# A chunked recurrence with a feed-forward block behind it: another order of operations, a spread by 128-row products, whole-half stores and an early flag

## The chip, the cores and the metric

One core of one Trainium2 chip runs the whole kernel. The metric is device time in microseconds (us) of that core, as the median of several runs. The engines are TensorE (PE, products; its weight loads are listed as PEld), VectorE (DVE), ScalarE (ACT), GpSimd (POOL) and SyncE (SP, which here issues nearly all transfers). Everything is float32.

## What is computed

```python
# r, k, v, w, a, b: (batch 4, heads 8, 768 tokens, 40)
state = zeros((B, H, D, D))
for t in range(S):
    y[:, :, t] = einsum('bhd,bhde->bhe', r_t, state)
    Sa = einsum('bhde,bhe->bhd', state, a_t)
    state = state * w_t[:, :, None, :] - einsum('bhd,bhe->bhde', Sa, b_t)
    state = state + einsum('bhd,bhe->bhde', v_t, k_t)
x = y as (B*S = 3072 tokens, H*D = 320)
h = x @ w_in                  # 320 -> 2048
out = (h * sigmoid(h)) @ w_out    # 2048 -> 320
```

## The kernel before

The 768 tokens are cut into 12 chunks of 64. Within a chunk the recurrence is turned into products and the inverse of a triangular matrix for each of the 32 pairs of batch and head, so that the state moves on once for each chunk. The feed-forward block of a chunk (256 tokens over the four batches) then follows.

The work is a list of some 1400 operations, each of one engine. They are written down by steps: `prepare(n)` (DVE scans L476 and L494 for the decays, scaling L503, the second operand L507, products L526, their mask L591, turning by L631, products L606), `special(n)` for the first two chunks (the triangular inverse on DVE and PE: dots L657 and L658, the spread L734, gather L785, both L842, turn L855, products L887 and DVE sums L902, three rounds of them), `chain(n)` (L1041, L1051, solve L1066, L1096, L1126, L1153, L1169), `read(n)` (look L1199 with its mask L1211, L1238, L1253, scaling L1264), `bring(n)` (the transfer of the scaled result through `xh` to `xt`, L1283, L1344 and L1346), and `moe(n)` (L1356 and L1369 make 2048 features from 320, L1379 is the silu on ACT, L1396 is the second product in two output halves of four parts each, L1408 copies a half out of PSUM, L1411 stores it). `inverse(k)` and `merge(k)` (L968, L994) serve two later chunks together: its dots on DVE, transfers md to mi and zd to ZQ through DRAM, and then products with ZQ. `weights(u)` for u = 0 to 9 turns the 64-bit weights into float32 on DVE and ACT (L339 to L357), with products by L363 for the first three.

No scheduler sorts these steps when the program is built. The table `ORDER` lists all operations in one fixed sequence, and each engine gets its own in that sequence. The table `SLOTS` gives to each stretch of PSUM use one of four `pair` tiles or one of two `lam` tiles. An operation waits for the data that it reads and for the users of the tile that it overwrites. SP issues transfers in its own order as well, and where one waits, those behind it on SP wait too.

L734, the spread, takes the inverse's parts to another layout: for each of 16 positions, two products of 64 rows, with `fold` as the right operand, a view into the output buffer `ot`. ACT then copies the result to `xs` in one instruction.

There is a fallback: `guard()` counts on DVE how many entries of a check are in range, adds them over the partitions by one product (L1435), and writes a flag `bad` (L1438). All engines load the flag (L1488) and branch (L1489) around a slow general version. The guard is the last thing on the list, so DVE writes the flag behind the last copy.

Of the kernel before, what the change touches and what calls it, by code (L numbers as in the profile page):

```python
# [129 lines left out]
01001320111001013332100203211223101103303113201032131321222203130311323300300330021021001012012012122003033032  # L130
02110122311301200033321330210003311032122012123032031001303022012221221111213030021331311012031301020012032100
3301311002232331201021233230133211001311001001320012311102301202201130032012312121031300312032
# [4 lines left out]
def kernel(  # L137
# [69 lines left out]
    wc = ring("wc", 3, Q)  # L207
    ot = ring("ot", 1, DM)
    pairs = [ps.tile([128, 2, 512], F32, name=f"pair{i}") for i in range(4)]
    lams = ring("lam", 2, Q * C)  # L210
    ms, zs = (dr.tile([128, 16, 16], F32, name=x) for x in ("ms", "zs"))
    few = ZQ.rearrange("p q t -> p (q t)")
    fold, own, mine = ot[0][:, 288:304], ot[0][:, 304:308], ot[0][:, 308:312]
    xh = [dr.tile([DM, T], F32, name=f"xh{i}") for i in range(NN)]
    md = [dr.tile([128, 32, 32], F32, name=f"md{i}") for i in range(2)]
    xd = [dr.tile([128, 32, 32], F32, name=f"xd{i}") for i in range(2)]
    zd = [dr.tile([2, 32, 32, 32], F32, name=f"zd{i}") for i in range(2)]

    plan = Plan({"pair": pairs, "lam": lams})
# [1401 lines left out]
```

## Time and profile before

| what | us |
|---|---|
| three runs | 693.54, 689.51, 689.6 |
| median | 689.6 |
| profiled execution, whole | 695.31 |
| its span, first to last instruction | 693.3 |
| PE busy in it | 651.6 |
| DVE, ACT, POOL busy | 386.5, 209.4, 6.5 |
| largest groups on PE: L1396, L1356, L1369 | 220.7, 174.0, 47.3 |
| first product starts | 13.98 |
| last product of the kernel ends | 684.77 |

The profiled execution is 5.7 us above the median of the runs; its span leaves 2.0 us of its time outside. The parts of a profile used here are the page (busy shares, 40 slices of the span, the chain of work that ended last), a table of stages, the timeline of one engine, and groups of instructions by line. In a timeline row stand start, duration, engine, line, operation, destination and source, and in brackets the idle time before it with what ended it. A float32 product shows as two records, so "x8" of L1396 is four products. "issue" is time in which an engine waited for nothing that the profile shows.

### The profile page before, as it was taken

How to read it: one execution, taken by the hardware profiler on the slowest of the kernel's cores; microseconds unless marked ns; L12 is line 12 of the kernel's file. 1: busy time of each engine (PE TensorE's matmuls, PEld its weight loads, DVE VectorE, ACT ScalarE, POOL GpSimd, SP SyncE). 2: the span in 40 equal slices, each digit the busy share in tenths (PEclk: the TensorE clock that was granted, in tenths of full speed). 3: DMA queues.
4: the chain of work that ended last, by engine and by line, in shares of the span. 5: the costliest groups of instructions: out<-in, count | busy, mean ns of one | idle time of the engine just before them, and what ended most of it. 6: DMA issues, size and time to landing. Idle time of an engine off the chain costs nothing.

```text
span 693.3 us, 26090 instructions
## 1 busy us (share of the span) xinstructions
PE 651.6 (94%) x12150; PEld 521.7 (75%) x12150; DVE 386.5 (56%) x558; ACT 209.4 (30%) x285; POOL 6.5 (1%) x21
## 2 busy tenths in 40 slices
PE   1799997999999999999999999999989999999995
PEld 1576785787788787888688788788778787787773
DVE  7899988798353952665934727961628611202000
ACT  4455535034324033323034224044113033131020
POOL 2000000100000000000000000000000000000000
PEclk9999999999999999999999999999999999999998
DMA  9934756426453254542734651453350431301001
GB/s 323 276 82 128 195 156 191 127 77 139 119 131 95 61 152 97 150 105 64 160 94 105 178 119 57 124 135 81 90 117 24 121 93 31 92 13 50 16 8 23
DMA packets 113711, 76.27 MB, mean 110 GB/s; under 512 B 61884, under 2 KB 109820, under 8 KB 112956
## 3 DMA queue, kind: packets, MB, share of 16 engines
q1 hardware_dynamic: 113596, 74.54, 41.1%
q8 instruction: 96, 1.57, 1.0%
q14 instruction: 19, 0.16, 0.1%
HBM read 60.16 MB, written 14.35 MB: 107 GB/s over the span
## 4 chain that ended last, share of the span: by engine, by line
PE 83%; DMA 7%; SPq 4%; DVE 2%; issue 2%; ACT 1%; DVEq 0%
PE pair L1396 28%; PE pair L1356 22%; PE pair L1369 6%; PE pair L1199 4%; PE pair L1253 3%; PE pair L526 3%; PE pair L363 2%; PE pair L1153 2%; DMA vu<-in_v 2%; PE pair L606 2%; PE pair L631 2%; PE pair L1238 2%; PE pair L1041 2%; PE pair L1066 1%; DMA kbv<-in_bT 1%
## 5 line engine op out<-in xcount | busy, mean ns | idle before, releaser
L1396 PE MATMUL pair<-wo,gts 128*128 128x320 f32 x768 | 220.7, 441 | 2.1 <-issue 2.1
L1396 PEld LDWEIGHTS pair<-wo,gts 128*128 128x128 f32 x768 | 143.6, 191 | 59.8 <-issue 4.0
L1356 PE MATMUL pair<-xt,wi 128*128 128x256 f32 x768 | 174.0, 383 | 1.6 <-DMA xt<-xh 1.6
L1356 PEld LDWEIGHTS pair<-xt,wi 128*128 128x128 f32 x768 | 144.5, 191 | 23.4 <-DVE XI L657 2.0
L1379 ACT ACTIVATE gts<-pair 128x1024 f32<-128x1024 f32 x48 | 47.3, 1020 | 60.7 <-PE pair L1369 59.8
L1211 DVE TENSOR_TENSOR lam<-pair,ml 128x1024 f32<-128x1024 f32 x22 | 26.2, 1220 | 69.7 <-PE pair L1199 69.7
L658 DVE TENSOR_REDUCE XI<-XI 128x64 f32<-128x512 f32 (+9 forms) x85 | 58.7, 690 | 2.9
L657 DVE TENSOR_TENSOR XI<-XI,mi 128x1024 f32<-128x1024 f32 (+8 forms) x60 | 33.6, 560 | 41.7 <-DMA mi<-md 40.5
L1408 DVE COPY ot<-pair 128x320 f32<-128x320 f32 x24 | 11.7, 486 | 74.1 <-PE pair L1396 65.0
L1369 PE MATMUL pair<-xt,wi 64*128 64x256 f32 x384 | 47.3, 387 | 0.0
L526 PE MATMUL pair<-a,kb 40*64 40x64 f32 x1536 | 28.8, 228 | 15.7 <-DVE a L503 14.0
L526 PEld LDWEIGHTS pair<-a,kb 40*64 40x64 f32 x1536 | 26.1, 142 | 19.5 <-issue 16.5
L1369 PEld LDWEIGHTS pair<-xt,wi 64*128 64x128 f32 x384 | 35.3, 189 | 4.9 <-issue 1.0
L507 DVE TENSOR_TENSOR kb<-kbv 128x1024 f32<-128x1024 f32 x24 | 29.1, 1216 | 10.8 <-DMA kbv<-in_kT 5.3
L1199 PEld LDWEIGHTS pair<-r,vut 40*64 40x64 f32 x1536 | 24.9, 136 | 10.0 <-issue 7.4
L1199 PE MATMUL pair<-r,vut 40*64 40x64 f32 x1536 | 27.2, 222 | 5.1 <-issue 2.8
L253 ACT COPY vu<-pair 64x640 f32<-64x640 f32 x22 | 15.1, 687 | 55.0 <-PE pair L1096 54.7
L930 ACT COPY mi<-XI 128x1024 f32<-128x1024 f32 x5 | 10.0, 1992 | 62.6 <-DVE XI L658 59.8
L476 DVE TENSOR_TENSOR_SCAN kbv<-wz,zt 128x1024 f32<-128x1024 f32 x12 | 27.5, 2292 | 1.0
L494 DVE TENSOR_TENSOR_SCAN wz<-wz,zt 128x1024 f32<-128x1024 f32 x12 | 27.4, 2285 | 0.1
L644 ACT COPY kt<-pair 128x640 f32<-128x640 f32 x24 | 16.3, 693 | 31.0 <-PE pair L631 30.9
L657 DVE TENSOR_TENSOR XI<-XI,xs 128x1024 f32<-128x1024 f32 (+1 forms) x25 | 25.2, 1008 | 0.6
(154 smaller groups left out, 637.3 us busy)
## 6 DMA issues: line engine op xcount, KB each, us to landing
wz<-in_wT SPq DMA_DIRECT2D x12, 512.0 KB
a<-in_aT SPq DMA_DIRECT2D x12, 512.0 KB
kbv<-in_bT SPq DMA_DIRECT2D x12, 512.0 KB
kbv<-in_kT SPq DMA_DIRECT2D x12, 512.0 KB
vut<-in_vT SPq DMA_DIRECT2D x48, 96.0 KB
r<-in_rT SPq DMA_DIRECT2D x48, 96.0 KB
vu<-in_v SPq DMA_DIRECT2D x24, 160.0 KB
out<-ot SPq DMA_DIRECT2D x48, 80.0 KB
```

The lines of the kernel that those rows point to most:

```text
L476: nc.vector.tensor_tensor_scan(back(V), back(W[:, 2 : 2 + Q * C]), zt, 1.0, ALU.mult, ALU.add)
L494: nc.vector.tensor_tensor_scan(Z, Z, zt, 0.0, ALU.mult, ALU.add)
L507: TTn[engine].tensor_tensor(out=at_(kb, m0, (m1 - m0, 2), (2 * C, 8), (1, C)), in0=at_((kf, bf)[is_b], 0, (8 * C, 2), (C, 8), (1, C)), in1 ...
L526: nc.tensor.matmul(room.tile[half(h), j, g * C : g * C + C], lhsT=kb[rows(j), place(is_b, q) : place(is_b, q) + C], rhs=A[rows(j), q * C : ...
L657: nc.vector.tensor_tensor(out=at_(tmp, 0, *dims), in0=x, in1=y, op=ALU.mult)
L658: nc.vector.tensor_reduce(out=out_, in_=at_(tmp, 0, *dims), axis=AX.X, op=ALU.add)
L1199: nc.tensor.matmul(pl.tile[half(1 - m if role else m), b, c * C : c * C + C], lhsT=vut[rows(b), role, hu, :], rhs=rs[rows(b), hh, :], star ...
L1211: lambda pl=pl, la=la: nc.vector.tensor_tensor(out=la.tile.rearrange("p (q t) -> p q t", q=Q), in0=pl.tile.rearrange("p a b -> p (a b)").r ...
L1356: nc.tensor.matmul(rooms[g].tile[:, f // 2, (f % 2) * T : (f % 2) * T + T], lhsT=wi[:, k, (4 * g + f) * 128 : (4 * g + f) * 128 + 128], rh ...
L1369: nc.tensor.matmul(rooms[g].tile[:, h, (f % 2) * T : (f % 2) * T + T], lhsT=wi3[half(h), g * 256 + (f % 2) * 128 : g * 256 + (f % 2) * 128 ...
L1379: nc.scalar.activation(out=gts[:, 4 * g * T : 4 * g * T + 4 * T], in_=rooms[g].tile.rearrange("p a b -> p (a b)"), func=AF.Silu)
L1396: nc.tensor.matmul(po[b].tile[:, 0, 0:DM], lhsT=g4[:, f, 128 * b : 128 * b + 128], rhs=wo[:, f, :], start=f == 0, stop=f == NF - 1,)
```

## The change

`ORDER` and `SLOTS` are new, the result of another search (1418 operations before, 1395 now). Five edits come with them.

1. The spread does 16 products over all 128 rows in place of 32 products over 64. `fold` gets a tile of its own of 128 x 2 x 16, zero outside two blocks (one more memset on POOL, two sums over 64 partitions on DVE for one over 128). The result stands in the lower 64 partitions, and two ACT copies of 64 x 256 bring it to `xs`.
2. `own` and `mine`, two other small operands, move within `ot`.
3. Each output half goes out in one transfer of 160 KB in place of two of 80 KB, so 24 stores for 48.
4. The guard is listed ahead of the third part of the last output half, and that part is made to depend on the flag.
5. The last output half is copied by ACT and its store is issued by ACT.

Lines of the kernel after are 4 to 10 higher than before for the same operation.

```diff
 ORDER = """
-0 6 2 1 102 127 7 9 8 10 14 103 128 3 11 17 15 25 129 104 16 26 130 18 105 41 106 27 139 71 67 114 4 115 65 5 63 131
+0 6 128 1 3 2 7 129 8 9 10 130 14 11 131 12 13 15 23 25 71 103 284 4 104 132 77 133 105 106 27 26 24 134 17 115 116
...
-    fold, own, mine = ot[0][:, 288:304], ot[0][:, 304:308], ot[0][:, 308:312]
+    own, mine = ot[0][:, 288:292], ot[0][:, 292:296]
+    fold = sb.tile([128, 2, 16], F32, name="fold")
...
+        nc.gpsimd.memset(fold, 0.0)
+        for b in range(2):
+            x = ident[half(b)].rearrange("p (g s) -> p s g", s=16)
+            nc.vector.tensor_reduce(out=fold[half(b), b], in_=x, axis=AX.X, op=ALU.add)
...
                 for t in range(16):
-                    for b in range(2):
-                        nc.tensor.matmul(
-                            pr.tile[half(b), 0, 16 * t : 16 * t + 16],
-                            lhsT=at_(XI[half(b)], 64 * t, (1, 64)),
-                            rhs=fold[half(b)],
+                    nc.tensor.matmul(
+                        pr.tile[half(0), 0, 32 * t : 32 * t + 32],
+                        lhsT=at_(XI, 64 * t, (1, 64)),
+                        rhs=fold.rearrange("p b s -> p (b s)"),
...
-                lambda: nc.scalar.copy(
-                    out=xs.rearrange("p (s t) -> p s t", s=16), in_=pr.tile[:, 0, 0:256].rearrange("p (t s) -> p s t", t=16)
-                ),
+            for b in range(2):
...
+                    lambda b=b: nc.scalar.copy(
+                        out=xs[half(b)].rearrange("p (s t) -> p s t", s=16),
+                        in_=pr.tile[half(0), 0].rearrange("p (t b s) -> p b s t", t=16, b=2)[:, b],
+                    ),
...
-            add("DVE", vec(320), lambda b=b: nc.vector.tensor_copy(out=ot[0], in_=po[b].tile[:, 0, 0:DM]), [po[b]], ["ot"], 10 * n, [po[b]])
-            for m in range(2):
-                r0 = (2 * m + b) * S + C * n
-                dma(lambda m=m, r0=r0: nc.sync.dma_start(out[r0 : r0 + C, :], ot[0][half(m)]), 80, ["ot"], [("out", n, b, m)], 10 * n + 9)
+                if n == NN - 1 and b == 1 and part == 2:
+                    guard()
+                last_ = ["bad"] if n == NN - 1 and b == 1 and part == 2 else []
...
+            e = "ACT" if n == NN - 1 and b else "DVE"
+            add(e, vec(320), lambda b=b, e=e: copy(e, ot[0], po[b].tile[:, 0, 0:DM]), [po[b]], ["ot"], 10 * n, [po[b]])
+            dst = out.rearrange("(m b s) c -> b m s c", m=2, b=2)[b, :, C * n : C * n + C]
+            q = nc.scalar if e == "ACT" else nc.sync
+            dma(lambda q=q, dst=dst: q.dma_start(dst, ot[0]), 160, ["ot"], [("out", n, b)], 10 * n + 9, "ACT" if e == "ACT" else "SP")
...
-    guard()
```

What the new order does is seen at three places. In the rows, a number behind a tile's name is its buffer (`a_82` belongs to chunk 3 here, `a_84` to chunk 2), and "x16" counts instructions.

The first is DVE between the second and the third sum of `special(1)`, L902 before (L908 after), where `prepare(3)` is also under way. Before:

```order
L902 TENSOR_TENSOR XI<-pair_113,X_94 128x1024
L494 SCALAR_TENSOR_TENSOR wz_73<-wz_73,zt 128x1024
L495 MEMSET zt 128x16
L339 TENSOR_SCALAR wo<-wo 128x1024
L503 TENSOR_TENSOR a_82<-a_82,wz_73 128x1024
L342 TENSOR_SCALAR raw_136<-raw_136 128x1024
L507 TENSOR_TENSOR kb<-kbv 128x2x8x64
L902 TENSOR_TENSOR X_94<-pair_111,X_94 128x1024
```

And after:

```order
L908 TENSOR_TENSOR XI<-pair_111,X_94 128x1024
L346 TENSOR_SCALAR raw_137<-raw_137 128x1024
L343 TENSOR_SCALAR wo<-wo 128x1024
L478 TENSOR_SCALAR w_77<-wz_73,pad 128x16
L479 MEMSET wz_73 128x16
L480 SCALAR_TENSOR_TENSOR kbv<-wz_73,zt 128x1024
L908 TENSOR_TENSOR X_94<-pair_113,X_94 128x1024
L345 SCALAR_TENSOR_TENSOR wo<-raw_137,wo 128x1024
```

The second scan of `prepare(3)` (L494), its scaling (L503) and one of its L507 stood ahead of the third sum; only the first scan (L480, which was L476) stands there now, and the rest of that step comes later.

The second is PE in the same stretch, from the third round of `special(1)` to the first L1396 (L1402 after) of the first feed-forward block. Before:

```order
L1356 MATMUL pair_110<-xt,wi 128x256 x8
L887 MATMUL pair_111<-XI 64x64 x32
L631 MATMUL pair_113<-ident,kb 128x40 x16
L1369 MATMUL pair_112<-xt,wi_67 128x256 x4
L1369 MATMUL pair_110<-xt,wi_67 128x256 x4
L526 MATMUL pair_113<-a_82,kb 64x64 x32
L1066 MATMUL pair_111<-X_94,R_91 40x64 x32
L1199 MATMUL pair_112<-r,vut 64x64 x32
L1199 MATMUL pair_113<-r,vut 64x64 x32
L1396 MATMUL pair_111<-wo,gts 128x320 x4
```

And after:

```order
L893 MATMUL pair_113<-XI 64x64 x32
L1362 MATMUL pair_111<-xt,wi 128x256 x8
L1072 MATMUL pair_112<-X_94,R_91 40x64 x32
L635 MATMUL pair_113<-ident,kb 128x40 x16
L1375 MATMUL pair_110<-xt,wi_67 128x256 x4
L1375 MATMUL pair_111<-xt,wi_67 128x256 x4
L1205 MATMUL pair_112<-r,vut 64x64 x32
L1205 MATMUL pair_113<-r,vut 64x64 x32
L1402 MATMUL pair_111<-wo,gts 128x320 x8
```

The block of L1356 moved from ahead of the third L887 to behind it, the turn (L631) and the remainder of the features (L1369) moved from ahead of the solve (L1066) to between it and the look (L1199), and the L526 of chunk 3 is now behind the first L1396.

The third is the end of SP's list. Before:

```order
L1344 DMA xt<-xh_129 128x2x256
L1411 DMA out<-ot_109 64x320
L1346 DMA xt<-xh_129 64x256
L1411 DMA out<-ot_109 64x320 x2
L1346 DMA xt<-xh_129 64x256
L1411 DMA out<-ot_109 64x320 x6
L1488 TENSOR_LOAD bad
L1488 ISA x2
L1489 COMPARE_AND_BRANCH
```

And after:

```order
L1289 DMA xh_130<-lam_114 40x4x256 x2
L1497 TENSOR_LOAD bad
L1497 ISA x2
L1350 DMA xt<-xh_130 128x2x256
L1352 DMA xt<-xh_130 64x256
L1421 DMA out<-ot_109 2x64x320
L1352 DMA xt<-xh_130 64x256
L1421 DMA out<-ot_109 2x64x320 x2
L1498 COMPARE_AND_BRANCH
```

The load of the flag moved from behind all stores to ahead of the last loads of `xt` and the last three stores that SP issues; the last store of all is no longer SP's.

More of the change, by code (lines that the diff above doesn't have):

```diff
@@ L74 @@
 ORDER = """
[52 rows of a table removed]
[51 rows of a table added]
 """
 SLOTS = """
-01001320111001013332100203211223101103303113201032131321222203130311323300300330021021001012012012122003033032
-02110122311301200033321330210003311032122012123032031001303022012221221111213030021331311012031301020012032100
-3301311002232331201021233230133211001311001001320012311102301202201130032012312121031300312032
+03032120310310103031113322130113030313031321012120133302233203100302120300030113122221301002313031103311122222
+00100132320321013011100300311032300031101031201111110203120312213322011300113010023031121123130320221101023303
+2001230013120210211030030211133011012222110103012320100322011112102101010220331321031101320133
 """
@@ L286, in once @@
             nc.gpsimd.tensor_copy(out=ot[0][rows(j), 112 + D * j : 112 + D * j + D], in_=ident[rows(j), rows(j)])
-        for x, axes in ((fold, "p (g s) -> p s g"), (own, "p (b c s) -> p c b s"), (mine, "p (g c) -> p c g")):
-            sizes = dict(s=16) if x is fold else dict(b=2, c=4) if x is own else dict(c=4)
+        nc.gpsimd.memset(fold, 0.0)
+        for b in range(2):
+            x = ident[half(b)].rearrange("p (g s) -> p s g", s=16)
+            nc.vector.tensor_reduce(out=fold[half(b), b], in_=x, axis=AX.X, op=ALU.add)
+        for x, axes in ((own, "p (b c s) -> p c b s"), (mine, "p (g c) -> p c g")):
+            sizes = dict(b=2, c=4) if x is own else dict(c=4)
             nc.vector.tensor_reduce(out=x, in_=ident.rearrange(axes, **sizes), axis=AX.XY if x is own else AX.X, op=ALU.add)
@@ L725, in special @@
         turned = few[:, 256:512]
-        xsk = ["xs"]
+        xsk = [("xs", 0), ("xs", 1)]
         if n in RELAY:
@@ L732, in spread @@
                 for t in range(16):
-                    for b in range(2):
-                        nc.tensor.matmul(
-                            pr.tile[half(b), 0, 16 * t : 16 * t + 16],
-                            lhsT=at_(XI[half(b)], 64 * t, (1, 64)),
-                            rhs=fold[half(b)],
-                            start=True,
-                            stop=True,
-                        )
-            add("PE", 1.9, spread, XIk, [pr], pri, [pr], 64)
-            add(
-                "ACT",
-                act(256),
-                lambda: nc.scalar.copy(
-                    out=xs.rearrange("p (s t) -> p s t", s=16), in_=pr.tile[:, 0, 0:256].rearrange("p (t s) -> p s t", t=16)
-                ),
-                [pr],
-                ["xs"],
-                pri,
-                [pr],
-            )
+                    nc.tensor.matmul(
+                        pr.tile[half(0), 0, 32 * t : 32 * t + 32],
+                        lhsT=at_(XI, 64 * t, (1, 64)),
+                        rhs=fold.rearrange("p b s -> p (b s)"),
+                        start=True,
+                        stop=True,
+                    )
+            pr.left = 3
+            add("PE", 1.9, spread, XIk, [pr], pri, [pr], 64)
+            for b in range(2):
+                add(
+                    "ACT",
+                    act(256),
+                    lambda b=b: nc.scalar.copy(
+                        out=xs[half(b)].rearrange("p (s t) -> p s t", s=16),
+                        in_=pr.tile[half(0), 0].rearrange("p (t b s) -> p b s t", t=16, b=2)[:, b],
+                    ),
+                    [pr],
+                    [("xs", b)],
+                    pri,
+                    [pr],
+                )
         else:
@@ L758, in special @@
                 [("ms", b, c) for b in range(2) for c in range(4)],
-                ["xs", ("in", "S", n)],
+                [*xsk, ("in", "S", n)],
                 pri,
@@ L1406, in moe @@
                 need = sorted({("wo", c) for c in range(4 * part * DM // WS, ((4 * part + 4) * DM - 1) // WS + 1)})
-                add("PE", 2.14, partial(second, b, part), [("gts", part), ("ff", n), *need], [po[b]], pri + 4 + b + part * 0.1, [po[b]], 16, shape="F")
-            add("DVE", vec(320), lambda b=b: nc.vector.tensor_copy(out=ot[0], in_=po[b].tile[:, 0, 0:DM]), [po[b]], ["ot"], 10 * n, [po[b]])
-            for m in range(2):
-                r0 = (2 * m + b) * S + C * n
-                dma(lambda m=m, r0=r0: nc.sync.dma_start(out[r0 : r0 + C, :], ot[0][half(m)]), 80, ["ot"], [("out", n, b, m)], 10 * n + 9)
+                if n == NN - 1 and b == 1 and part == 2:
+                    guard()
+                last_ = ["bad"] if n == NN - 1 and b == 1 and part == 2 else []
+                add("PE", 2.14, partial(second, b, part), [("gts", part), ("ff", n), *need, *last_], [po[b]], pri + 4 + b + part * 0.1, [po[b]], 16, shape="F")
+            e = "ACT" if n == NN - 1 and b else "DVE"
[3 more added lines that the diff above has]
+            dma(lambda q=q, dst=dst: q.dma_start(dst, ot[0]), 160, ["ot"], [("out", n, b)], 10 * n + 9, "ACT" if e == "ACT" else "SP")
     def ahead(step, n):
```

101 rows, old and new, of the table ORDER are left out of this document.

## The prediction

> **What bounds the kernel now.** I read the page first: the busy shares, the tenths and the chain that ended last.
>
> ```profile
> PE 651.6 (94%) x12150; PEld 521.7 (75%) x12150; DVE 386.5 (56%) x558; ACT 209.4 (30%) x285; POOL 6.5 (1%) x21
> PE   1799997999999999999999999999989999999995
> DVE  7899988798353952665934727961628611202000
> PE 83%; DMA 7%; SPq 4%; DVE 2%; issue 2%; ACT 1%; DVEq 0%
> ```
>
> TensorE (PE) is busy 94% of the span. Only PE work taken away, or idle PE time closed, can shorten this kernel. The 1 in PE's first slice, the 7 in its second and seventh and the 5 in its last show where idle time lies. Beside the first and the seventh, VectorE (DVE) shows 7 to 9: DVE sets the pace there. So I cut the span into stages (busy time of PE, PEld, DVE, ACT, POOL, then granted clock, DMA share, GB/s).
>
> ```profile
> 0.00:14.00 14.00, 0.02 (x3) 0.05 (x3) 10.15 (x29) 5.14 (x5) 4.05 (x17) 1.00 0.90 308
> 14.00:52.00 38.00, 31.69 (x764) 25.01 (x768) 33.87 (x56) 19.93 (x26) 0.00 (x0) 1.00 0.74 197
> 52.00:83.00 31.00, 30.93 (x618) 23.03 (x612) 30.16 (x51) 16.88 (x23) 0.52 (x1) 1.00 0.59 159
> 83.00:119.00 36.00, 28.66 (x680) 24.82 (x681) 30.38 (x36) 16.12 (x19) 0.00 (x0) 0.91 0.60 178
> 340.00:510.00 170.00, 164.61 (x3274) 132.05 (x3273) 92.47 (x124) 51.23 (x75) 0.00 (x0) 0.99 0.46 115
> 684.70:693.30 8.60, 0.09 (x2) 0.00 (x0) 0.54 (x2) 0.00 (x0) 0.00 (x0) 0.69 0.13 28
> ```
>
> PE's idle time is 14.0 us before the first product, 6.3 up to 52, 7.3 between 83 and 119, 5.4 between 340 and 510, and 8.5 behind the last product: 41.5 of the 41.7 us that PE is not busy (693.3 - 651.6). Any gain has to come out of these five places or out of PE's own work.
>
> **The change, part by part.** *Tile-shape changes.* Four products of L1396 between blocks of their own shape, and between others, in the chain:
>
> ```profile
> 245.68 2.15 PE pair L1396 x8
> 161.64 2.35 PE pair L1396 x8
> ```
>
> A change of shape at both ends costs 0.20 us. I counted the places in PE's row of work where the tile's shape changes: 211 before, 211 after. The new order only shifts them among shapes, with changes into 128x128 falling from 73 to 62 and into 64x128 rising from 40 to 47. I take 0; the bounds are plus or minus 1 us (ten changes at 0.10).
>
> *The spread.* Thirty-two products of 64 rows (64 records) against sixteen of 128 rows; for the new ones the nearest row is L1253, which also has 128 rows and 64 records:
>
> ```profile
> 18.10 3.59 PE L734 MATMUL pair<-ot,XI 64*64 64x16 f32 x64
> 227.32 1.79 PE pair L1253 x64
> ```
>
> By L1253, sixteen products take half of 1.79, or 0.9; by L734's own pace they would take 1.8. I take 0.9, 2.7 less than now. It lies at 18 us, where DVE paces the work (33.9 of 38 us busy), so on the end it gives 0, at most 2.7. In place of one copy ACT does two, and DVE does two half-height sums for one; what they add at 18 us (under 1 us) lies in the same place, and I net it with the spread's gain.
>
> *The order between 83 and 119 us.* This is where most of it must come from. PE, then DVE:
>
> ```profile
> 83.40 0.69 PE L855 MATMUL pair<-ident,mi 64*128 64x64 f32 x16
> 85.20 1.16 PE L842 MATMUL pair<-mi,sb 64*64 64x64 f32 x64 [1.11 <-ACT X L253]
> 87.49 3.43 PE L887 MATMUL pair<-X,XI 64*64 64x64 f32 x62 [1.13 <-ACT XI L253]
> 97.51 3.72 PE L1356 MATMUL pair<-xt,wi 128*128 128x256 f32 x16
> 101.16 2.08 PE L887 MATMUL pair<-XI 64*64 64x64 f32 x64
> 103.69 1.97 PE L1369 MATMUL pair<-xt,wi 64*128 64x256 f32 x16
> 106.88 1.16 PE L526 MATMUL pair<-a,kb 40*64 40x64 f32 x64 [1.22 <-DVE kb L507]
> 107.93 1.10 PE L1066 MATMUL pair<-X,R 64*40 64x64 f32 x64
> 110.18 1.61 PE L1199 MATMUL pair<-r,vut 40*64 40x64 f32 x91 [1.04 <-ACT vut L255]
> 114.63 1.14 PE L1199 MATMUL pair<-r,vut 40*64 40x64 f32 x33 [2.84 <-issue]
> 115.70 4.59 PE L1396 MATMUL pair<-wo,gts 128*128 128x320 f32 x12
> ```
>
> ```profile
> 91.03 1.23 DVE L902 TENSOR_TENSOR XI<-pair,X 128x1024 f32<-128x1024 f32 x1 [1.56 <-PE pair L887]
> 97.63 1.23 DVE L902 TENSOR_TENSOR XI<-pair,X 128x1024 f32<-128x1024 f32 x1 [0.85 <-PE pair L887]
> 98.77 2.28 DVE L494 TENSOR_TENSOR_SCAN wz<-wz,zt 128x1024 f32<-128x1024 f32 x1
> ...
> 105.51 1.22 DVE L507 TENSOR_TENSOR kb<-kbv 128x1024 f32<-128x1024 f32 x1 [1.99 <-DMA kbv<-in_bT]
> 106.66 1.22 DVE L902 TENSOR_TENSOR X<-pair,X 128x1024 f32<-128x1024 f32 x1
> ```
>
> The third L902 could have run at 103.2, when the third L887 ended; it ran at 106.7, because the scan of L494, the L503 after it and an L507 that waits 1.99 us for a load stand ahead of it on DVE. Now they stand behind it. I follow the new order on PE. Ahead of L855 a block of L1369 (2.0) and one of L631 (0.5) are gone, and the block before may start up to 2.0 earlier, so L855 runs at 78.9 to 80.9. From there to the first L902 it is 7.6 as before, and 0.9 more because a block of L1369 now stands in the wait of 1.13: 87.4 to 89.4, and I take 88.4. Then L1356 (3.7) and L887 (2.1): second L902 at 94.2. L631 and L526 (1.6) cover it, then L887: product ready at 97.9. DVE, with a scan still ahead, gets to the third L902 at 99.3. PE does an L1356 meanwhile and reaches L1066 at 101.6, with no wait. L631, L1369 (0.5 and 2.0) now stand between L1066 and L1199, and cover the wait of 1.04. L1396 then starts at 101.6 + 1.1 + 2.5 + 2.0 = 107.2, against 115.70. One L526 block (1.07) that was ahead comes later: the lead is 8.5 - 1.1 = 7.4, and 7 as I take it. If the 2.84 us stop, for which the trace shows no releaser ("issue"), comes back, it is 4.6; if L855 is at its early end and L1396 runs at its usual pace (12 records 3.5 instead of 4.59), 9.5. Bounds 4.6 to 9.5.
>
> The clock in this stage was 0.91, and the L1396 behind the 2.84 us stop is 1.1 us slow. The Trainium skill, "TensorE: Matmul & The Clock Gate", Part 1, has the clock fall to half after an idle window of about 3.4 us. Here a stop of 2.84 us, with 1.04 some 1.6 us before it, was enough. By the page's rule stops under 3.4 us would leave the clock whole, and the sum would be 1.1 us lower; the trace does not bear that out.
>
> *The later order.* Idle time between 340 and 510 is a load and one more such stop:
>
> ```profile
> 337.41 8.17 DMA xt<-xh
> 504.00 2.15 issue
> ```
>
> I find as much PE work between L1253 and the next L1356 after the change as before, or more, so I leave these 5.4 us as they are: plus or minus 4.
>
> *Stores.* Half as many issues on SP; SP is not on the path outside the last stage, so 0.
>
> *The end.* Copy, the two stores' issue, flag load, SP's wait for its own branch, and the DMA share in the second after:
>
> ```profile
> 684.77 0.49 DVE L1408 COPY ot<-pair 128x320 f32<-128x320 f32 x1 [5.97 <-PE pair L1396]
> 685.29 1.11 SPq L1411 DMA_DIRECT2D out<-ot  x2
> L1488 SPq TENSOR_LOAD <-bad x1: 737/737/737, 686.5 to 686.5; - x1
> SPq L1489 <- SPq L1489: 2.5, 1, 2.5
> 686.50:687.50 1.00, 0.00 (x0) 0.00 (x0) 0.00 (x0) 0.00 (x0) 0.00 (x0) 1.00 0.78 172
> ```
>
> The chain is copy, issues 1.11, flag load 0.74 behind them, branch 2.5, and then 3.2 us of closing waits. Now SP loads the flag long before the end and has no last store to issue, so its branch can be done early. ACT copies (no row of ACT for this size; I take DVE's 0.5, at most 0.7) and issues (half of 1.11): 1.2 us after PE's end. The data move mostly up to 687.5, which is 2.2 us after the first issue and 1.7 after the second's start; I take 2.5. With the 3.2 of closing waits that makes 6.9 instead of 8.6. I take a gain of 2; the bounds are 0.5 (ACT pays the branch of 2.5 too, behind its flag load) and 3.5 (part of the closing waits overlaps).
>
> Two waits are added there. SP's load of the flag stands ahead of the last loads of xt and of three stores. The flag follows one tiny DVE operation behind the last L1264, which the transfers to xh ahead of it on SP wait for anyway, so 0. PE's third part of the last output half now waits for the flag as well, with more than 30 us of L1356, L1369 and L1396 between the flag's product and it, so 0. There is one buffer ot: ACT's copy has to wait until the store of the other half has read it, and only 4.5 us of L1396 (eight products, 16 records) lie between the two copies at the least. Against copy, issue and 2.2 us for the data (3.3) that holds with about 1 us to spare; should it not, some tenths of the gain go.
>
> The Trainium skill, "DMA: Bandwidth & Descriptors", "Issuing engines are not separate DMA queues", says that issuing from another engine only saves the sequencer's issue time. By that alone the sum's last term would be 0.6. In the rows above the flag load of 0.74 and the branch of 2.5 stood behind the issue on SP too, which is why I take more.
>
> **Sum.** -7 (start) + 0 (shapes) + 0 (spread) + 0 (later) - 2 (end) = -9. The profiled execution took 695.3 us (span 693.3 and 2.0 outside), which is 5.7 above the median of 689.6; I apply the difference to the median: 680.6.
>
> **Rivals.**
> *The lead is eaten by a new wait.* The next thing late would be the merge of the inverse:
>
> ```profile
> 129.81 0.16 DVE L657 TENSOR_TENSOR XI<-XI,mi 128x4 f32<-128x4 f32 x1
> 168.81 0.75 PE L968 MATMUL pair<-ZQ,sb 32*32 32x32 f32 x64
> ...
> L968 PE MATMUL pair<-ZQ,sb 32*32 32x32 f32 x640 | 7.5, 194 | 0.5 <-DMA ZQ<-zd 0.5
> ```
>
> That chain takes up to 39.0 us from its first dot to L968. After the change PE gets to L968 at 107.2 + 53.1 (as from 115.7 to 168.8) = 160.3. PE ends the block that L1264 waits for some 8 us after L1396's start (4.5 of L1396 and about 3.4 of three small blocks), and eight other DVE operations of about 1 us each follow L1264 before the dots, which so start near 124.5. With two weight steps fewer among the dots (2.3 us) the chain ends near 161. It is level, so a small slip in the load of mi or of the weights makes PE wait. If that or the stop of 2.84 takes 4 to 5 of the 7 us, the time is 685 (683 to 688), within 1%. Chance 0.25.
>
> *The change doesn't do what it says.* It counts shape changes, and they are as many as before; if DVE's order matters less than I read, only the end gains: 687.6. Chance 0.08.
>
> *Slower.* The five merges all come late. Summing the durations of PE's blocks between them, the distance from an inverse's last L526 to its merge falls from 56 to 46 us for the first and from 62 to 52 for the second. If each of five merges waits over 1.8 us, the gain of 9 is gone; at 4 us each it is 20 - 9 = 11 slower, 700. Against it: before, L968 waited 0.5 us in all. Chance 0.08.
>
> **How the numbers follow.** My forecast, 680.6, has 0.59, its own range is 676 to 684. The range of 8 in 10 is 674 (lead 9.5, end 3.5, later idle 3 less) to 689.5, which takes in the first two rivals. One per cent, 6.9 us, is about what a measurement of this kernel can tell from no change: under 682.7 is faster. From my forecast nearly all (0.56) and a little of the first rival (0.04) lie there: 0.60; slower 0.08; the rest 0.32.
>
> **What would show it.** Right: the first L1396 starts near 107 (105 to 111); the third L902 ends before PE's L1356 does; PE's idle time between 83 and 119 falls from 7.3 to under 3; 510 on stays solid; behind the last product 6 to 7 us. Wrong: a PE wait on ZQ at the first L968, a long "issue" ahead of L1396, or L855 waiting for mi. A PE busy time that fell by more than 3 us would show that shape changes did matter.

## The result, and the profile after

The kernel after takes 715.98 us (median; 715.12 to 721.07) against 689.63 us before: a ratio of 1.038, with a 95% interval of 1.033 to 1.043. It is slower by 3.8%. A ratio here is an estimate over the fast runs of both kernels, and need not be the quotient of two medians. The profiled execution took 715.12 us, with a span of 713.4.

The busy shares and the slices of the page of the kernel after:

```profile
PE 658.7 (92%) x12118; PEld 529.4 (74%) x12118; DVE 384.5 (54%) x558; ACT 210.0 (29%) x287; POOL 6.3 (1%) x22
PE   1979999999998999989999899988999999999993
PEclk9999999999999999989999899998999999999998
```

PE is busy for 7.1 us more (658.7 against 651.6) and idle for 54.7 us (713.4 - 658.7) instead of 41.7. Between its first and last slice the kernel before had three slices under 9, two of them near the start (the 2nd and the 7th). Now five slices with an 8 are scattered from the 13th to the 28th. Two stages of the kernel before that are needed beside those shown above, and then the stages of the kernel after:

```profile
170.00:340.00 170.00, 169.85 (x3546) 136.98 (x3545) 96.38 (x140) 50.59 (x76) 0.00 (x0) 1.00 0.45 109
510.00:684.70 174.70, 174.70 (x2482) 139.44 (x2480) 46.84 (x64) 33.77 (x45) 0.00 (x0) 1.00 0.20 52
```

```profile
83.00:119.00 36.00, 34.45 (x771) 28.52 (x768) 34.31 (x40) 20.92 (x24) 0.00 (x0) 1.00 0.62 184
170.00:340.00 170.00, 161.28 (x3357) 132.20 (x3358) 94.52 (x136) 47.51 (x71) 0.00 (x0) 0.96 0.42 109
340.00:510.00 170.00, 162.40 (x3121) 131.18 (x3122) 85.33 (x113) 47.21 (x68) 0.00 (x0) 0.96 0.42 107
510.00:705.00 195.00, 188.28 (x2683) 149.38 (x2674) 53.11 (x77) 37.12 (x51) 0.00 (x0) 1.00 0.20 52
705.00:713.40 8.40, 0.00 (x0) 0.00 (x0) 0.00 (x0) 0.00 (x0) 0.00 (x0) 0.59 0.07 20
```

Between 83 and 119 us PE's idle time fell from 7.3 to 1.6 us and the clock rose to 1.00: the start got better. From 170 us on PE loses 8.7, 7.6 and 6.7 us in stages that had lost 0.2, 5.4 and 0 before (of the 6.7, 2.5 lie behind its last product, which ends at 702.5). In the first two of them the granted clock is 0.96, where it had been 1.00 and 0.99. The timeline of PE after, at the place that carried the sum:

```profile
99.23 1.10 PE L1072 MATMUL pair<-X,R 64*40 64x64 f32 x64
104.95 1.20 PE L1205 MATMUL pair<-r,vut 40*64 40x64 f32 x66 [1.10 <-issue]
106.08 4.57 PE L1402 MATMUL pair<-wo,gts 128*128 128x320 f32 x16
```

The first L1402 starts at 106.1, where L1396 started at 115.7. So the lead was won, and lost later. The waits of DVE name where. In the table of waits stand engine, line and releaser, total, number and the longest one; before, then after:

```profile
DVE ot L1408 <- DMA out<-ot: 8.9, 2, 5.5
```

```profile
DVE ot L257 <- DMA out<-ot: 47.0, 8, 10.0
```

L257 is now the line of the copy into `ot`. It waits for the store of the half before it, 47.0 us in all. DVE's waits as such cost nothing where PE has work. But PE now waits for that very copy four times, 4.6 us in all, which the table of the kernel before does not have:

```profile
PE pair L974 <- DVE ot L257: 1.7, 1, 1.7
PE pair L1362 <- DVE ot L257: 1.4, 1, 1.4
...
PE pair L1205 <- DVE ot L257: 1.1, 1, 1.1
...
PE pair L635 <- DVE ot L257: 0.4, 1, 0.4
```

The timelines of DVE and SP after show one such store from end to end, in a quiet place:

```profile
670.78 0.49 DVE L257 COPY ot<-pair 128x320 f32<-128x320 f32 x1 [21.07 <-issue]
677.13 0.49 DVE L257 COPY ot<-pair 128x320 f32<-128x320 f32 x1 [5.86 <-DMA out<-ot]
```

```profile
671.30 0.58 SPq L1421 DMA_DIRECT2D out<-ot  x1
```

From the issue at 671.30 to the release of `ot` at 677.13 pass 5.8 us. The view of the DMA engines from 671 to 678 us, in 40 slices of 0.175 us (tenths of the 16 engines busy), tells how:

```profile
DMA  0000000011012571111110111111111110000000
```

Apart from a short burst, the load of `xt`, one tenth of the sixteen engines is busy for four microseconds: about two engines pass the 128 rows of 1280 bytes one after another.

The trace also keeps the time of each update of the semaphores by which transfers report that they have landed. They bear out the two engines for this store, and show what it does to a transfer behind it. A transfer of 64 rows (in the kernel with two stores, below) makes 16 updates. This one makes three: one at 672.26, ahead of the first slice in which an engine is busy, and two at 677.00 and 677.01. The load of `xt` that SP issued right behind it, at 671.97, makes 14 of its 16 updates between 673.83 and 675.04 and the last two at 677.30 and 677.32, just behind the store's two. In the kernel with two stores the same load was issued at 650.44 and had all 16 by 652.67. So two parts of a load that has nothing to do with the store stand behind it: the load lands after 5.3 us in place of 2.2.

### The profile page after: what moved, and what is told of

It is laid out like the page before. It is cut to its first block, busy times and chain, and to the rows that moved or that the text cites. A ratio compares the mean times of both kernels' runs of the same rounds, so it can differ in the third digit from the quotient of the medians.

```text
span 713.4 us, 26003 instructions
## 1 busy us (share of the span) xinstructions
PE 658.7 (92%) x12118; PEld 529.4 (74%) x12118; DVE 384.5 (54%) x558; ACT 210.0 (29%) x287; POOL 6.3 (1%) x22
## 5 line engine op out<-in xcount | busy, mean ns | idle before, releaser
L1402 PE MATMUL pair<-wo,gts 128*128 128x320 f32 x768 | 219.6, 441 | 0.1
L1402 PEld LDWEIGHTS pair<-wo,gts 128*128 128x128 f32 x768 | 144.5, 192 | 58.8 <-issue 2.9
L1362 PE MATMUL pair<-xt,wi 128*128 128x256 f32 x768 | 175.5, 386 | 3.6 <-DMA xt<-xh 2.2
L1362 PEld LDWEIGHTS pair<-xt,wi 128*128 128x128 f32 x768 | 146.1, 192 | 26.1 <-DVE ot L257 1.8
L257 DVE COPY ot<-pair 128x320 f32<-128x320 f32 x23 | 11.2, 488 | 101.2 <-DMA out<-ot 47.0
L1375 PE MATMUL pair<-xt,wi 64*128 64x256 f32 x384 | 49.0, 398 | 0.0
L1205 PE MATMUL pair<-r,vut 40*64 40x64 f32 x1536 | 28.7, 230 | 7.5 <-DMA r<-in_rT 4.4
L1205 PEld LDWEIGHTS pair<-r,vut 40*64 40x64 f32 x1536 | 26.5, 144 | 11.5 <-issue 9.0
L480 DVE TENSOR_TENSOR_SCAN kbv<-wz,zt 128x1024 f32<-128x1024 f32 x12 | 27.5, 2292 | 1.0
L253 ACT COPY X<-pair 32x256 f32<-32x256 f32 (+2 forms) x43 | 16.7, 389 | 33.5 <-PE pair L1000 33.1
L522 ACT ACTIVATE kbv<-kbv 128x1024 f32<-128x1024 f32 x12 | 12.7, 1058 | 43.5 <-DVE kb L511 43.5
```

The costliest lines, as they stand in the source:

```text
L253: nc.scalar.copy(out=dst, in_=src)
L480: nc.vector.tensor_tensor_scan(back(V), back(W[:, 2 : 2 + Q * C]), zt, 1.0, ALU.mult, ALU.add)
L1205: nc.tensor.matmul(pl.tile[half(1 - m if role else m), b, c * C : c * C + C], lhsT=vut[rows(b), role, hu, :], rhs=rs[rows(b), hh, :], star ...
L1362: nc.tensor.matmul(rooms[g].tile[:, f // 2, (f % 2) * T : (f % 2) * T + T], lhsT=wi[:, k, (4 * g + f) * 128 : (4 * g + f) * 128 + 128], rh ...
L1375: nc.tensor.matmul(rooms[g].tile[:, h, (f % 2) * T : (f % 2) * T + T], lhsT=wi3[half(h), g * 256 + (f % 2) * 128 : g * 256 + (f % 2) * 128 ...
L1402: nc.tensor.matmul(po[b].tile[:, 0, 0:DM], lhsT=g4[:, f, 128 * b : 128 * b + 128], rhs=wo[:, f, :], start=f == 0, stop=f == NF - 1,)
```

## The experiments

The kernel before measured 689.6 us in the comparison with the kernel after and 692 to 695 in those below, so the ratios within a comparison are what is read.

**Two stores per half again.** Only the store is undone; the order, the spread, the flag and ACT's last store stay.

```diff
-            dma(lambda q=q, dst=dst: q.dma_start(dst, ot[0]), 160, ["ot"], ...)
+            def store(q, b=b):
+                for m in range(2):
+                    r0 = (2 * m + b) * S + C * n
+                    q.dma_start(out[r0 : r0 + C, :], ot[0][half(m)])
+            dma(lambda q=q, store=store: store(q), 160, ["ot"], ...)
...
```

> The kernel after, with each output half stored by two transfers of 64 rows again (same place in the order, the last pair still issued by ACT). Theory A (the one transfer per half lands late: its 128 packets of 1280 bytes come one after another on two DMA engines, some 5.7 to 6.3 us from issue to release, and DVE's next copy into the only buffer ot waits for it with everything behind it): the store lands in about 2.2 us again, DVE's wait on out<-ot falls from 47.0 us to under 10, PE's extra time after 166 us falls from 38 to about 10, and the time is 680 to 688. Theory B (the new order itself makes PE wait for loads, looks and merges, and the store only happens to be in the way): 705 to 716, with PE's waits where they are now.

It took 687.8 us, 0.990 of before (0.980 to 0.999): at the upper end of what theory A expected, and far from theory B. Its profiled execution has a span of 683.7. The same late store pair in this kernel, DVE and then the DMA engines from 648.7 to 655.7 us, again in slices of 0.175 us:

```profile
648.71 0.49 DVE L257 COPY ot<-pair 128x320 f32<-128x320 f32 x1 [21.06 <-issue]
652.00 0.49 DVE L257 COPY ot<-pair 128x320 f32<-128x320 f32 x1 [2.80 <-DMA out<-ot]
```

```profile
DMA  0000000003960784025310000000595179100000
...
out<-ot SPq DMA_DIRECT2D x4, 80.0 KB, 2.1
```

The engines are now busy in bursts of 6 to 9 tenths, a store lands 2.1 us after its issue, and the copy waits 2.8 us instead of 5.9. But one expectation missed: DVE's wait on the store is still 19.9 us in all, not under 10. With two issues behind one another and one buffer the copies remain close, but PE's table of waits no longer has a row for the copy.

```profile
DVE ot L257 <- DMA out<-ot: 19.9, 6, 7.2
```

**The slow store in the old order.** The kernel before, with the first of a half's two store operations left empty and the second one issuing 2 x 64 rows.

```diff
...
-                dma(lambda m=m, r0=r0: nc.sync.dma_start(out[r0 : r0 + C, :], ot[0][half(m)]), 80, ...)
+                dma(lambda m=m, dst=dst: m and nc.sync.dma_start(dst, ot[0]), 80, ...)
```

> The kernel before, with its old order, and each output half stored by one transfer of 2 x 64 rows at the place of the second of its two. Theory A: DVE's wait on out<-ot grows from 8.9 us to 30 or more and the time to 700 to 720, since this order leaves the copies no more room for a store of some 6 us. Theory B: the wait grows by the few us that the place costs, and the time stays within 1% of 689.6.

It took 702.09 us. DVE's wait grew as expected of theory A, but the time only to 1.010 of before (1.005 to 1.015), which theory B would allow as well:

```profile
DVE ot L1408 <- DMA out<-ot: 34.3, 9, 7.1
```

So the slow store costs 1% in the old order, and 4.9% in the new one (1.038 / 0.990). The order decides how much of it is seen. In this kernel's profile PE waits 1.8 us for the copy and 7.6 us for loads, where the kernel before has 0 and 7.4; why the old order leaves so much more room is not shown.

**Size or layout.** Two transfers of 80 KB, each with half the columns of all 2 x 64 rows (the edit is shown against the kernel with two stores).

```diff
-                for m in range(2):
-                    r0 = (2 * m + b) * S + C * n
-                    q.dma_start(out[r0 : r0 + C, :], ot[0][half(m)])
+                dst = out.rearrange("(m b s) c -> b m s c", m=2, b=2)[b, :, C * n : C * n + C]
+                for c in (slice(0, DM // 2), slice(DM // 2, DM)):
+                    q.dma_start(dst[:, :, c], ot[0][:, c])
```

> As e1_two_stores, two transfers of 80 KB per half, but each takes half of the columns of all 2 x 64 rows, where e1 took all columns of 64 rows. Theory A (it is the layout: a destination whose outermost dimension counts 2 is carried by two of the sixteen DMA engines): both transfers are slow, 5 us or more from issue to release, the DMA engines' mean busy share stays at one or two tenths during a store, and the time is 705 or more. Rival D (it is the size: 160 KB take longer than 80): as fast as e1, 682 to 692.

723.42 us in a single run, beside 694.82 for the kernel before, and DVE's waits on the store grew further:

```profile
DVE ot L257 <- DMA out<-ot: 53.4, 8, 10.7
```

So the size of a transfer is not the cause. By the semaphore updates of one such pair (issued at 707.29 and 707.84), each transfer again makes two late updates, and the two land 3.9 and 5.3 us after their issues, the second behind the first; 80 KB as 64 rows land in 2.0 or 2.1. Under 5 us for the first was not expected, but the pair keeps `ot` as long as one transfer of 160 KB (the copies at 638.20 and 685.64 wait 6.0 and 6.1 us). It is the layout, with its two pieces outermost. The Trainium skill, "DMA: Bandwidth & Descriptors", section "Why a DMA increments its semaphore by 16 and not by 1", says the same: the number of engines is the largest one up to 16 that divides the slowest dimension of both access patterns, which makes 2 here (pieces 2, partitions 128) and 16 for 64 rows. The one tenth of busy engines above and the two late updates agree.

**A buffer for each half.** The slow store stays; the second half is copied into a free stretch of a staging tile.

```diff
     raws = ring("raw", 1, 2 * WS)
+    outs = [ot[0], raws[0][:, 0:DM]]
...
-            add(e, vec(320), lambda b=b, e=e: copy(e, ot[0], po[b].tile[:, 0, 0:DM]), ...)
+            add(e, vec(320), lambda b=b, e=e: copy(e, outs[b], po[b].tile[:, 0, 0:DM]), ...)
...
```

> The kernel after, with its slow one transfer per half, but the second half of each chunk is copied into a buffer of its own (a stretch of the weights' staging tile, unused by then). Theory A (what costs is that the next copy waits for the store in the only buffer): a store still takes 5.7 to 6.3 us, but DVE's wait on out<-ot falls from 47 us to under 10 and the time to 682 to 692, near the kernel with two stores. Rival C (what costs is the store's place in SP's queue or its share of the DMA engines, not the buffer): the time stays above 700.

No wait on a store is left in DVE's table, but the time is 706.65 us, 1.021 of before (1.017 to 1.024). Theory A's time missed, and theory C was right that something besides the buffer costs. The waits of PE in this kernel:

```profile
PE pair L1206 <- DMA r<-in_rT: 3.0, 2, 1.7
...
PE pair L1376 <- DMA xt<-xh: 2.7, 1, 2.7
PE pair L975 <- DMA ZQ<-zd: 2.5, 2, 2.3
...
PE pair L1363 <- DMA xt<-xh: 1.7, 1, 1.7
...
PE pair L1206 <- DMA vut<-in_vT: 0.9, 1, 0.9
```

PE waits 10.8 us for four kinds of loads, none of which reads what the stores write.

**Both mends.** Two buffers and two stores per half.

> The kernel after with both mends: two transfers of 64 rows per half and a buffer for each half. Theory A: no DVE wait on out<-ot of more than 2 us is left; the time is that of the kernel with two stores alone or up to 4 us less (0.985 to 0.99 of before). Rival C: no different from two stores alone.

687.37 us, 0.991 of before (0.986 to 0.996), no DVE wait on a store, and one row of waits of PE for loads:

```profile
PE pair L1363 <- DMA xt<-xh: 1.8, 2, 1.4
```

That is just above the 0.985 to 0.99 that theory A expected, and no better than two stores alone (0.990). With fast stores these runs show nothing that the second buffer still gives.

**A slow transfer that nobody waits for.** To the kernel with both mends, each half that SP stores gets one more transfer of its 160 KB to a spare place: in the slow layout, or, as a control, as two transfers of 64 rows.

```diff
+    spare = dr.tile([B * S, DM], F32, name="spare")
...
+                if q is nc.sync:
+                    q.dma_start(spare.rearrange("(m b s) c -> b m s c", m=2, b=2)[b, :, C * n : C * n + C], outs[b])
```

> The kernel with both mends (two buffers, two 64-row stores per half), and behind each half's stores that SP issues one more transfer of the same 160 KB in the slow layout (2 x 64 rows) to a spare place in DRAM that nobody reads. No copy waits for it, since each buffer rests some 40 us. Theory G (a transfer that sits on two DMA engines for about 5 us also holds up the parts of later transfers that those engines carry, which is what was left with two buffers and the slow store): PE waits for r, xt, vut or ZQ again (8 us or more in all), and the time is 1.015 to 1.03 of before. Rival H (what was left came from something else): within 0.5% of the kernel without it, 0.987 to 0.996 of before.

> The control: the same spare 160 KB per half, written as two transfers of 64 rows. It adds the same bytes, one more issue per half, and no long stay on two engines. Theory G: 0.987 to 1.0 of before, PE's waits for loads as without it (about 2 us). Rival H says nothing else; a rival by which added bytes or issues on SP matter would put it as high as e9_idle_slow_store.

With the slow one the kernel is as slow as the kernel after: 719.57 us, 1.040 of before (1.033 to 1.046), more than the 1.015 to 1.03 that theory G expected. The control is at 697.67 us, 1.009 (1.005 to 1.013), also above what was expected of it: the bytes and issues themselves cost some 1.8% of the kernel without them (1.009 / 0.991), and the layout another 3.1% (1.040 / 1.009). PE's waits for loads with the slow one, and then in the control:

```profile
PE pair L1207 <- DMA r<-in_rT: 6.2, 3, 2.6
PE pair L976 <- DMA ZQ<-zd: 4.3, 2, 3.0
...
PE pair L1377 <- DMA xt<-xh: 3.4, 2, 2.8
PE pair L1207 <- DMA vut<-in_vT: 2.4, 1, 2.4
PE pair L1364 <- DMA xt<-xh: 2.3, 2, 1.5
```

```profile
PE pair L1364 <- DMA xt<-xh: 2.4, 2, 1.5
...
PE pair L1207 <- DMA r<-in_rT: 0.6, 1, 0.6
...
PE pair L976 <- DMA ZQ<-zd: 0.4, 1, 0.4
...
PE pair L1377 <- DMA xt<-xh: 0.3, 1, 0.3
```

The first five rows make 18.6 us, those of the control 3.7. Theory G holds in its mechanism: a transfer that sits on two engines delays the loads issued after it. The semaphore updates of both traces say so without PE's waits. From 130 us on, the transfers other than stores that SP issued within 5 us behind a slow spare transfer (66 of them) landed after 5.85 us in the median, those behind a spare transfer of 64 rows in the control (74) after 3.01. For all the others the medians are 3.23 and 3.34. The trace does not number the engines; that the last two updates of the `xt` load above come just behind the store's own two is the nearest that it shows.

**The end, edit by edit.** From two stores per half, once with the last half copied by DVE and stored by SP, once with the flag made at the end.

```diff
-            e = "ACT" if n == NN - 1 and b else "DVE"
+            e = "DVE"
```

> Two stores per half and one buffer, as in e1_two_stores, with the last half copied by DVE and stored by SP again; the flag stays early. In e1_two_stores 4.9 us pass from the last product to the end, against 8.6 before. If most of that gain comes from ACT having the last store, this comes back to 7 to 8.6; if it comes from the early flag (SP's load of it and its branch no longer behind the stores), it is 5 to 6.

```diff
-... 1388 ... 1389 ... 1390 ... (ORDER)
+... 1388 ... 1389 1390
-                last_ = ["bad"] if n == NN - 1 and b == 1 and part == 2 else []
+                last_ = []
```

> As e1_two_stores, with ACT's last copy and store kept, but the flag's product and comparison at the end of the order again and no dependence of the last part on the flag. If the gain at the end comes from the early flag, 7 to 8.6 us pass from the last product to the end; if it comes from ACT's store, 5 to 6.

A single run each, 683.74 and 691.31 us; single times differ by more than this edit is worth, so I read the end alone. The last copy with the early flag alone, and then with ACT's store alone, in the timelines of DVE and ACT:

```profile
675.71 0.49 DVE L257 COPY ot<-pair 128x320 f32<-128x320 f32 x1 [3.81 <-PEq L1502]
```

```profile
681.91 0.43 ACT L253 COPY ot<-pair 128x320 f32<-128x320 f32 x1 [16.18 <-PE pair L1402]
```

From the start of the last copy to the end of the span pass 8.5 us before (684.77 to 693.3), 4.9 with both edits (678.85 to 683.7 with two stores), 6.3 with the early flag alone (675.71 to 682.0) and 7.6 with ACT's store alone (681.91 to 689.5). The flag brings 2.2, ACT's store 0.9, and both 3.6: each helps, and most comes from the flag. The 6.3 lies between the two ranges that were expected of it, the 7.6 in the one that speaks for the flag. In the kernel after it is 9.0 (704.41 to 713.4), and the copy itself had to wait for the other half's slow store: PE's last product had ended 1.9 us before it, and the store, issued at 698.78, made its last update at 704.31.

**The spread on two halves of PSUM's partitions.** The sixteen products write the two halves of PSUM's partitions in turn, and four copies collect them.

```diff
-                        pr.tile[half(0), 0, 32 * t : 32 * t + 32],
+                        pr.tile[half(t % 2), 0, 32 * (t // 2) : 32 * (t // 2) + 32],
...
```

> As e1_two_stores, with the sixteen spread products going to the two halves of PSUM's partitions in turn (and four copies of ACT for two). The spread took 3.5 us as 32 products of 64 rows before and 3.5 as 16 products of 128 rows after. Theory E (a product into the same columns of the array as the one before cannot overlap it, about 0.11 us a record, and two column tiles in turn halve that): it takes 1.7 to 1.9 us. Rival F (0.22 us is the price of a product of 128 rows and 64 columns): 3.5 us again. Either way the time stays at 683 to 690, since the spread lies where DVE sets the pace; the start of the first L1402 moves by less than 1 us.

The spread in the kernel after, and here:

```profile
18.43 3.60 PE L737 MATMUL pair<-fold,XI 128*64 128x32 f32 x32 [0.46 <-ACT kbv L523]
```

```profile
18.53 1.92 PE L737 MATMUL pair<-fold,XI 128*64 128x32 f32 x32 [0.46 <-ACT kbv L523]
```

Theory E holds but for 0.02 us: 1.92 where 1.7 to 1.9 was expected. The kernel took 690.15 us in a single run beside 694.82 for before, and the first L1405 (that kernel's L1402) started at 108.0, 1.9 later than with two stores alone, where under 1 us was expected; what delayed it is not shown. Whatever the spread's 1.7 us are worth, a single run cannot show it: those with two stores alone lie between 683.8 and 691.7.

## Why the prediction was wrong

It forecast 680.6 us, faster by 9, and got 26 more than before. The sum's terms, one by one:

*Start: right.* Forecast -7, from a first L1396 at 107.2; it started at 106.1. L855's successor ran at 79.5 (forecast 78.9 to 80.9), the third sum at 97.2 (99.3), L1066's successor at 99.2 (101.6). An "issue" stop of 1.1 us inside the look, which the sum had at 0, took back part of these 2.4. The lead at the first second product was 9.6 less the block of 1.1 that comes later, 8.5. PE's idle time from 83 to 119 us is 1.6, and "under 3" was asked for.

*Later order: within its bounds, as far as one profiled execution of each kernel tells.* With two stores PE's last product ends at 678.8, 5.9 us before that of the kernel before; so 2.6 of 8.5 were lost on the way. The forecast was 0, plus or minus 4. The merge, the first rival's mechanism, did not come late with two stores: the stop there is for `xt`, behind it.

*Shapes: not settled by itself.* PE is busy 649.2 us with two stores, 2.4 less than before, under the 3 us that was to speak against my count; the clock (0.993 against 0.989) is in that figure too.

*Spread: wrong size, no consequence.* I took 0.9 us from L1253; it took 3.6, as before. L1253 writes the two halves of PSUM's partitions by turns and these sixteen products do not; the experiment shows that this is the difference. The term on the end was 0, and stays so.

*End: right mechanism, too small.* Forecast -2 with bounds of 0.5 and 3.5; with two stores it is -3.6, just outside. In the kernel after, with the slow store, the end is 0.5 longer than before, not shorter.

*Stores: the step that failed.* "Half as many issues on SP; SP is not on the path outside the last stage, so 0." I priced the issue and not the transfer. Where I did use a landing time, at the end, I took the 2.2 us of the old 64-row stores for a transfer of another layout, and so found "about 1 us to spare" at the only place where I looked at the one buffer `ot`. The new store takes 5.8 us. With two stores of 64 rows the other terms give 0.990 of before, where -9 of 689.6 would be 0.987; nearly the whole error is that one term. None of the prediction's signs of being wrong looked at a store, and none of them came: PE waited 0.4 us for ZQ at the merge, the "issue" inside the look ahead of L1402 was 1.1 us, and L855's successor ran on time. Its sign that 510 us on stays solid failed. The slow store costs 4.9% (1.038 against 0.990), by two routes. The copy waits for the buffer and holds DVE with everything behind it: with a buffer for each half 1.7 points of the 4.8 are gone (1.038 to 1.021). The rest, 3.0 points (1.021 to 0.991), is about what a slow transfer costs that no copy waits for (3.1% against the control), and there the loads behind it come late.

The Trainium skill's table "Rules for kernel authors" in "DMA: Bandwidth & Descriptors" advises one 128-partition transfer in place of two to halves of the partitions. Here the two measure 2.1 us and the one 5.8, since the destination of the one has two pieces outermost; the same table has a row that warns of an outermost dimension below 16, and that is the row which applies.

The time also shows in PE's own work. Between the kernel after and that with two stores the span differs by 29.7 us: 20.2 of it are PE's idle time (54.7 against 34.5, that is 683.7 - 649.2), and 9.5 are PE's busy time (658.7 against 649.2), which is about what the granted clock accounts for, 0.976 in place of 0.993.

## What to carry to other kernels

Merging two transfers into one saves an issue and can cost far more: look at the outermost dimension of both sides, and read the landing time of a transfer of that very shape before its price is set to zero. A transfer that is slow because it sits on few engines harms twice, through whoever waits for its buffer and through the loads issued close behind it, so a second buffer alone does not mend it. The same slow store cost 1% in one order and 4.9% in another: the price of such an edit has to be taken in the order in which it will run.

## What was not expected of the hardware

Short stops of PE can cost more than their length. With two stores, a wait of 1.71 us behind the small products of a merge is followed by L1362 at a slow pace: the 23 records below (a block's first, as the view ends at 196 us) take 6.67 us, where 16 take 3.72 at 85.7 us, with no stop ahead, which is 5.3 for 23.

```profile
187.10 0.75 PE L974 MATMUL pair<-ZQ,sb 32*32 32x32 f32 x64
189.56 6.67 PE L1362 MATMUL pair<-xt,wi 128*128 128x256 f32 x23 [1.71 <-DMA xt<-xh]
```

The granted clock was 0.50 from 189.5 to 191.5 us and 0.74 for the two behind. It was 0.50 as well for 2 us from 114.7 us on in the kernel before, behind its stop of 2.84. Not every stop does it: in the kernel after, a stop of 1.10 us (104.95) is followed by L1402 at full pace, 16 records in 4.57 us. What decides it is not shown.

And products that write the same half of PSUM's partitions one after another cost 0.11 us a record (3.60 / 32), in two halves by turns 0.06 (1.92 / 32), whether over 64 or 128 rows: the 64 records of the old spread, in two halves by turns, took 3.59, which is 0.056.
